# Linear attention, mixer and gating on one core: the first MLP's side work ordered by a table

## The chip, the cores and the metric

The kernel runs on one core of a Trainium2 chip. The metric is device time in microseconds (us), the median of several executions. The engines are called by the names that the profile uses: PE (TensorE, matrix products), DVE (VectorE), ACT (ScalarE), POOL (GpSimd), and SP, which here only issues transfers. Each engine runs its own queue in the order in which the program was written; an instruction that waits holds up what is behind it on its engine.

## The reference

```python
for t in range(S):                       # B=4, H=8, S=768, D=48
    state = alpha[:, :, t, :, None] * state + einsum('bhd,bhe->bhde', k[:, :, t], v[:, :, t])
    y[:, :, t] = einsum('bhd,bhde->bhe', q[:, :, t], state)
x = y.transpose(0, 2, 1, 3).reshape(B, S, H * D)      # 768 x 384 for each of 4 batches
u = x + (x^T @ U @ V)^T                               # mixing over the sequence, rank 32
x = u + relu(u @ w_ch1) @ w_ch2                       # MLP, 384 -> 1536 -> 384
h = relu(x @ w_in);  a, v = halves of h               # 384 -> 1024
out = (a * (w_spatial @ layernorm(v) + b_spatial)) @ w_out
```

All inputs are float32. Products are made of high and low parts, three matmuls for one.

## The kernel before, in words

A batch has 768 rows, held transposed as two blocks of 384 columns. Its eight heads form four pairs, so that there are 16 pairs; pairs 0 to 3 are batch 0, pairs 4 to 7 batch 1. The attention of a pair goes in chunks of 64 rows. `prepare` (three parts, divided by `yield`) makes what depends on alpha alone: the backward scan on DVE (L691) with the scaling of k by POOL (L680) and a copy of the chunk products by ACT (L701); the forward scan (L703) with the scaling of q (L680); and ACT's check of alpha (L707), which reads alpha from the pair's input buffer, writes over the forward scan's tile, and sums into `over`. `Pair` then does the rest: the flip of k on PE (L732) and its copy kn by ACT (L735); `added`, the sums of k and v of each chunk (L775); `state`, with the decays and sums copied by ACT (L782, L783) and the scan over chunks by DVE (L786), in slices of DS columns; `keep` (L796, L797 on ACT); the scores (L748) and their mask (L757 on DVE); the outputs, in two kinds of products (L807 and L817), taken by ACT (L832). A pair's alpha, k and q lie together in one of three buffers, akq_84 to akq_86 in the program's names; pair n + 3 goes into the buffer of pair n, by `load_pair` (L634, two transfers, and L635 for v), as the last step of a pair.

`Mix` makes u: a flip of two halves (L947), ACT's copy of each, the product with U (L963), and its parts into stk (L971 on DVE); the sums with V follow (L291, added by DVE's L294, split by ACT's L295 into partuh and by L226 into partul).

The MLP goes over twelve pieces f of the hidden width. For a block and an f the up group makes nine matmuls (L351), ACT takes h (L358) and DVE the rest hl (L339); two groups later the down group makes three times three matmuls (L260 to L262) with h and hl, summed over some f in three banks, which DVE then adds to u (L409, three times). FIRST says in which ranges of f batch 0 goes. A piece of weights arrives as 64-bit words: DVE takes the high part (L215, L218), ACT scales the low part (L209), POOL adds (L221), ACT copies the high half (L562) and DVE the rest (L226).

Within a group PE's code calls `pull()` after every few matmuls, twice for an up group and four times for a down group. A pull runs the next steps of the work that goes beside the MLP: of `attend` for the next batch, and in batch 0 of the weights' conversion too. When a step is due is a formula: BEGINS and ENDS are the pulls at which a weight is begun and finished, `due()` spreads the steps of `attend` evenly over the pulls.

PSUM has eight banks: 0 to 2 for the down sums, 3 and 4 for the up groups, 5 to 7 ("x") for everything else, taken in turn.

Of the kernel before, what the change touches and what calls it, by code (L numbers as in the profile page):

```python
# [52 lines left out]
DS = 16  # L53
# [38 lines left out]
def gla_mixer_gating_kernel(ctx: ExitStack, tc: tile.TileContext, akq, v, vT, u, v3, w12, w_in, wsT, b_sp, w_out, out):  # L92
# [39 lines left out]
    class Stage:  # L132
# [4 lines left out]
        def __init__(self, pool, items, places=(), width=E, most=1):  # L137
            self.narrow = lambda: pool.tile([128, width], U32, name="narrow", tag="narrow", bufs=2)
            self.items, self.free = list(items), list(places)
            self.loaded, self.late, self.begun, self.most, self.scaled = [], [], 0, most, 0  # L140
# [30 lines left out]
        def begin(self, room=None):  # L171
# [6 lines left out]
            place, words, t, n, wide, finish = self.loaded.pop(0)  # L178
            if wide and not place:
                t = (room or self.narrow())[0 : words.shape[0], 0:n]  # L180
            if wide and not self.scaled:
                low_part(words)
            self.scaled = max(0, self.scaled - 1)
            x = narrowed(words, t) if wide else words
            self.late.append((self.begun, finish(x), place))
            self.begun += 1
            return True
# [23 lines left out]
    def narrowed(words, t):  # L211

        words = words.rearrange("p (n w) -> p n w", w=2)
        low, high = words[:, :, 0], words[:, :, 1]
# [5 lines left out]
        )  # L220
        nc.gpsimd.tensor_tensor(out=t, in0=t, in1=low, op=ALU.add)  # L221
# [85 lines left out]
    class ChannelMlp:  # L307
# [54 lines left out]
        def up_both(self, blocks, f):  # L362
# [14 lines left out]
            for ps in both:  # L377
# [5 lines left out]
                hs.append((h, hl))  # L383
            return hs
# [193 lines left out]
    with ExitStack() as fast:  # L578
# [7 lines left out]
        class Ps:  # L586
# [10 lines left out]
            def tile(self, shape, dtype, name, tag):  # L597
                return self.banks[:, self.place(tag), :]

            def two(self, tag):  # L600

                i, j = self.place(tag), self.place(tag)
                step = j - i
                last = j + (1 if step > 0 else -1)
                return self.banks[:, i : last if last >= 0 else None : step, :]
# [109 lines left out]
        class Pair:  # L715
# [7 lines left out]
            def flip(self, warm=0):  # L723
# [3 lines left out]
                for c0, c1 in ((0, 3), (3, NC)):  # L727
                    pt = ps.tile([128, 512], F32, "ps_kt", self.tags["flip"])
# [714 lines left out]
```

## Time and profile before

| what | value |
|---|---|
| median of 3 runs | 715.99 us (715.32 to 717.61) |
| the profiled execution | 716.3 us |
| its span, first to last instruction | 714.6 us |
| PE busy | 685.5 us, 96% |
| DVE, ACT, POOL busy | 341.0, 285.3, 203.1 us |
| mean granted clock of TensorE | 0.993 |
| chain that ended last | PE 82%, DVE 12%, ACT 3%, issue 2%, POOL 1% |

The times of the sections below come from the profiled execution, and the sum is made against its 716.3 us. PE is nearly always busy, so the views to read are those that tell where PE waits and at which clock it runs.

### The profile page before, as it was taken

To read this page: it belongs to the slowest core of one execution; us is meant where nothing else is said; L and a number is where in the kernel's file an instruction comes from. 1 tells how busy PE (TensorE), PEld (TensorE's weight loads), DVE (VectorE), ACT (ScalarE), POOL (GpSimd) and SP (SyncE) were. 2 spreads that over 40 slices of the span, in tenths; PEclk is the share of its full clock that TensorE was granted. 3 is DMA by queue.
4 is the path that set the end of the run, shared out by engine and by line. 5 is a ranking of instruction groups with operands and counts; after the bars stand their busy time and mean duration, and the time that the engine had idled before them with its cause. 6 is when DMAs were issued, how large, how long until landed. Compare 5 with 4: busy or idle time off the path is not lost.

```text
span 714.6 us, 14432 instructions
## 1 busy us (share of the span) xinstructions
PE 685.5 (96%) x6124; PEld 654.2 (92%) x6124; DVE 341.0 (48%) x584; ACT 285.3 (40%) x552; POOL 203.1 (28%) x172
## 2 busy tenths in 40 slices
PE   7989878999999999999999999999999999999996
PEld 6878867899999999989999999989999989999996
DVE  8998987556444335433233784352252143225211
ACT  3874446655455534454431543332231232214111
POOL 5534533215111031110030132343333223333211
PEclk9999999999999999999999999999999999999999
DMA  9699004442533310400004353400002003000001
GB/s 335 206 345 224 16 2 93 81 92 58 114 71 69 84 18 16 103 2 22 15 1 145 111 167 109 115 7 21 15 34 66 34 1 100 5 29 23 13 34 39
DMA packets 21178, 54.20 MB, mean 76 GB/s; under 512 B 2704, under 2 KB 12816, under 8 KB 19824
## 3 DMA queue, kind: packets, MB, share of 16 engines
q1 hardware_dynamic: 21104, 53.18, 27.2%
q8 instruction: 50, 0.82, 0.5%
q14 instruction: 24, 0.20, 0.1%
HBM read 42.55 MB, written 9.44 MB: 73 GB/s over the span
## 4 chain that ended last, share of the span: by engine, by line
PE 82%; DVE 12%; ACT 3%; issue 2%; POOL 1%; DMA 0%; DVEq 0%; ACTq 0%
PE banks L351 19%; PE banks L260 18%; PE banks L262 17%; PE banks L261 17%; PE banks L817 2%; DVE bw L691 2%; DVE narrow L215 1%; DVE fw L703 1%; PE banks L963 1%; PE banks L748 1%; PE banks L807 1%; DVE w L226 1%; PE banks L775 1%; PE banks L732 1%; PE banks L947 1%
## 5 line engine op out<-in xcount | busy, mean ns | idle before, releaser
L351 PE MATMUL banks<-partuh,w 128*128 128x384 f32 x564 | 131.0, 340 | 4.5 <-DVE hl L339 4.5
L351 PEld LDWEIGHTS banks<-partuh,w 128*128 128x128 f32 x564 | 100.5, 189 | 6.2 <-DVE hl L339 5.8
L339 DVE SCALAR_TENSOR_TENSOR hl<-banks,h 128x384 fp32r<-128x384 f32 x96 | 52.9, 552 | 103.4 <-ACT h L358 102.6
L260 PE MATMUL banks<-h,w 128*128 128x384 f32 x288 | 99.8, 347 | 0.9 <-DVE ub L409 0.9
L262 PE MATMUL banks<-hl,w 128*128 128x384 f32 x288 | 96.9, 337 | 0.0
L261 PE MATMUL banks<-h,w 128*128 128x384 f32 x288 | 96.9, 336 | 0.0
L511 DVE TENSOR_TENSOR vsb<-banks,bb 128x384 f32<-128x384 f32 x32 | 17.8, 558 | 129.6 <-PE banks L262 129.6
L358 ACT ACTIVATE h<-banks 128x384 fp32r<-128x384 f32 x94 | 45.9, 488 | 75.4 <-PE banks L351 74.4
L226 POOL TENSOR_TENSOR partul<-ub,partuh 128x384 fp32r<-128x384 f32 x45 | 46.0, 1048 | 91.8 <-ACT partuh L295 75.1
L517 ACT ACTIVATE gh<-gt 128x384 fp32r<-128x384 f32 x32 | 16.8, 525 | 126.3 <-DVE gt L514 126.3
L226 POOL TENSOR_TENSOR gl<-gt,gh 128x384 fp32r<-128x384 f32 x32 | 32.4, 1014 | 120.7 <-ACT gh L517 120.7
L261 PE MATMUL banks<-wsph,vl 128*128 128x384 f32 x192 | 65.1, 339 | 1.0 <-POOL vl L226 0.9
L351 PE MATMUL banks<-partul,w 128*128 128x384 f32 x282 | 66.1, 342 | 0.0
L260 PE MATMUL banks<-wsph,vh 128*128 128x384 f32 x192 | 64.9, 338 | 0.0
L262 PE MATMUL banks<-wspl,vh 128*128 128x384 f32 x192 | 64.9, 338 | 0.0
L260 PEld LDWEIGHTS banks<-h,w 128*128 128x128 f32 x288 | 54.4, 189 | 2.6 <-DVE ub L409 1.2
L261 PEld LDWEIGHTS banks<-h,w 128*128 128x128 f32 x288 | 54.5, 189 | 0.0
L262 PEld LDWEIGHTS banks<-hl,w 128*128 128x128 f32 x288 | 54.5, 189 | 0.0
L351 PEld LDWEIGHTS banks<-partul,w 128*128 128x128 f32 x282 | 50.0, 189 | 0.7
L680 POOL TENSOR_TENSOR akq<-akq,bw 128x768 f32<-128x768 f32 (+1 forms) x15 | 24.6, 1640 | 82.4 <-DVE bw L691 82.4
L680 POOL TENSOR_TENSOR akq<-akq,fw 128x768 f32<-128x768 f32 (+1 forms) x15 | 25.0, 1666 | 61.3 <-DVE fw L703 54.8
L226 POOL TENSOR_TENSOR vl<-vt,vh 128x512 fp32r<-128x512 f32 x20 | 27.1, 1382 | 49.8 <-ACT vh L481 49.8
(184 smaller groups left out, 1374.7 us busy)
## 6 DMA issues: line engine op xcount, KB each, us to landing
akq<-in_akq SPq DMA_DIRECT2D x24, 434.4 KB, 7.1
bits<-in_w SPq DMA_DIRECT2D x12, 768.0 KB, 12.3
x2d<-ub SPq DMA_DIRECT2D x8, 576.0 KB, 3.5
ub<-x2d SPq DMA_DIRECT2D x8, 576.0 KB, 4.9
out_y<-ob SPq DMA_DIRECT2D x24, 192.0 KB, 1.9
v<-in_v SPq DMA_DIRECT2D x15, 288.0 KB, 7.5
words<-in_w_in SPq DMA_DIRECT2D x8, 384.0 KB, 3.2
words<-in_wsT SPq DMA_DIRECT2D x4, 576.0 KB, 5.0
```

Source lines behind the costliest of these rows:

```text
L226: engine.tensor_tensor(out=out, in0=x, in1=hi.bitcast(F32), op=ALU.subtract)
L260: nc.tensor.matmul(out=ps, lhsT=wh, rhs=xh, start=first, stop=False)
L261: nc.tensor.matmul(out=ps, lhsT=wl, rhs=xh, start=False, stop=False)
L262: nc.tensor.matmul(out=ps, lhsT=wh, rhs=xl, start=False, stop=last)
L339: nc.vector.scalar_tensor_tensor(out=hl, in0=ps[:, 0:TB], scalar=0.0, in1=h.bitcast(F32), op0=ALU.max, op1=ALU.subtract)
L351: nc.tensor.matmul(out=ps[:, 0:TB], lhsT=wx[:, k * 128 : (k + 1) * 128], rhs=ux[:, k, :], start=i == 0, stop=i == len(parts) - 1)
L358: nc.scalar.activation(out=h, in_=ps[:, 0:TB], func=AF.Relu)
L511: nc.vector.tensor_tensor(out=vsb, in0=psv[:, 0:TB], in1=self.g["bb"][:, blk * TB : (blk + 1) * TB], op=ALU.add)
L517: nc.scalar.activation(out=hi, in_=gt, func=AF.Copy)
L680: engine.tensor_tensor(out=chunks(x)[:, c], in0=chunks(x)[:, c], in1=chunks(by)[:, c, 1:CW], op=ALU.mult)
L691: nc.vector.tensor_tensor_scan(out=bw[:, ::-1], data0=a[:, 1 : AW + 1][:, ::-1], data1=ends[:, ::-1], initial=0.0, op0=ALU.mult, op1=ALU.max)
L817: nc.tensor.matmul(out=self.py[HW * h : HW * h + D, x, j * CH : (j + 1) * CH], lhsT=self.w[:, c - 1, h, :], rhs=self.q[:, c * CH : (c + 1) ...
```

## The change

The diff is cut to its core; line numbers of the kernel before are used throughout, apart from the rows of the changed program below, in which L727 is the check L707, L585 is L562, L379 is L358, L755 is L735, L721 is L701, L852 is L832, L654 is L634, L655 is L635, L247 is L226, L360 is L339, L711, L714 and L723 are L691, L694 and L703, L232 and L235 are L215 and L218, L432 is L409 and L806 is L786.

```diff
-DS = 16
+DS = 8
...
-FIRST = (0, 5, 8, 12)
+FIRST = (0, 5, 8, 10, 12)
 N_WARM = 12
-BEGINS = (1, 9, 17, 25, 34, 43, 54, 65, 76, 87)
-AHEAD, N_AHEAD, HELD = 20, 5, 62
-ENDS = tuple(x + y for x in BEGINS for y in (10, 12))
+FIRST_STEPS = {
+    5: "f", 6: "b", 13: "fbf", 22: "fbf", 31: "fbf", 40: "fbf", 49: "fbf", 58: "f", 59: "pf", 67: "p",
+    70: "a", 72: "b", 73: "a", 77: "aa", 78: "fbf", 82: "a", 83: "ar", 84: "fpf", 91: "p", 92: "a", 95: "a", 97: "b",
+    99: "aa", 103: "fbf", 104: "a", 105: "a", 106: "r", 108: "fpf", 114: "p", 117: "a", 119: "pa", 121: "r", 122: "aa",
+    123: "p", 126: "a", 127: "aa", 129: "a", 130: "r", 131: "aa", 132: "p", 134: "a", 135: "a", 137: "a", 138: "a", 139: "p",
+    140: "a", 142: "a", 144: "a", 145: "ar",
+}
 BANKS = {"acc": 3, "mm": 2, "x": 3}
 PLACES = {"acc": (0, 1, 2), "mm": (3, 4), "x": (5, 6, 7)}
+PAIR = PLACES["x"][0:2]
+ALONE = PLACES["x"][2]
...
+        def high(self, room=None):
+
+            place, words, t, n, wide, finish = self.loaded.pop(0)
...
+            if wide:
+                high_part(words, t)
+            self.raised.append((place, words, t, wide, finish, self.scaled > 0))
+            self.scaled = max(0, self.scaled - 1)
+
+        def add(self):
+
+            place, words, t, wide, finish, scaled = self.raised.pop(0)
+            if wide and not scaled:
+                low_part(words)
+            x = both_parts(words, t) if wide else words
+            self.late.append((self.begun, finish(x), place))
+            self.begun += 1
...
+                if len(hs) == 1:
+                    self.pull()
...
-            def two(self, tag):
...
+            def pair(self):
+
+                return self.banks[:, PAIR[0] : PAIR[1] + 1, :]
...
-                for c0, c1 in ((0, 3), (3, NC)):
-                    pt = ps.tile([128, 512], F32, "ps_kt", self.tags["flip"])
+                for (c0, c1), tag in zip(((0, 3), (3, NC)), self.tags["flip"]):
+                    pt = ps.tile([128, 512], F32, "ps_kt", tag)
...
-                pts = [ps.tile([128, 512], F32, "ps_sc", self.tags["scores"]) for h in range(2)]
+                pts = [ps.tile([128, 512], F32, "ps_sc", PAIR[h]) for h in range(2)]
...
-                pd = ps.two(self.tags["state"])
+                pd = ps.pair()
...
-                decay = pd[:, 0, D * NC : D * NC + DS * NCH]
+                decay = pd[:, 0, TB : TB + DS * NCH]
...
-                    self.py = ps.two(self.tags["out"])
+                    self.py = ps.pair()
...
-        def attend(b, blocks):
-
-            tags = {"flip": "x", "scores": "x", "state": "x", "out": "x"}
+        checks = []
+
+        def prepare_some(ns):
+
+            for n in ns:
+                x = prepare(n)
+                next(x)
+                yield
+                next(x)
+                checks.append(x)
+                yield
+
+        def attend(b, blocks, alone=False):
+
+            tags = {"flip": (ALONE, PAIR[0])}
...
-                ahead = prepare(n + 1)
+                ahead = iter(()) if alone else prepare(n + 1)
                 pair.flip()
                 if mix:
-                    mix.take(mix.flip(0))
+                    mix.take(mix.flip(0, PAIR[1]))
                 yield
...
                 pair.state(pair.added())
                 if mix:
-                    mix.take(mix.flip(1))
+                    mix.take(mix.flip(1, ALONE))
...
                 pair.mask(pair.scores())
-                next(ahead, None)
...
                 if mix:
-                    gp = mix.product()
+                    gp = mix.product(0, ALONE)
                 pair.outputs()
...
                 if n + 3 < NPAIR:
                     load_pair(n + 3)
+                next(ahead, None)
...
+            if alone:
+                blocks += [(us[blk], *up.parts()) for blk in range(NB)]
+                for blk in range(NB):
+                    for m in range(KE - 1):
+                        mix_sum(g, blocks[blk], blk, m, stk, ps, "x")
+                    yield
+                    if blk == 0:
+                        mix.take(mix.flip(0))
+                        mix.take(mix.flip(1))
+                        yield
+                mix.keep(mix.product())
+                yield
+                for blk in range(NB):
+                    mix_sum(g, blocks[blk], blk, KE - 1, stk, ps, "x")
+                    yield
+                return
...
-            for m, blk, engine in (
-                (0, 0, nc.gpsimd), (0, 1, nc.gpsimd), (1, 0, nc.gpsimd), (2, 0, nc.vector), (1, 1, nc.vector), (2, 1, nc.vector)
-            ):
+            for blk in range(NB):
                 t, hi, lo = blocks[blk]
-                rest(lo[:, m, :], t[:, m, :], hi[:, m, :], engine)
-            weights.finish(1)
+                for m in range(KE):
+                    rest(lo[:, m, :], t[:, m, :], hi[:, m, :], nc.gpsimd if blk == m == 0 else nc.vector)
...
-        more = attend(1, nxt)
-        steps = chain(rest_of_first, more)
+        steps = attend(1, nxt, True)
+        ahead_of_1 = prepare_some(range(NP, 2 * NP + 1))
...
-            if b == 0 and pulls in ENDS:
-                weights.finish(1)
-            if b == 0 and pulls in BEGINS:
-                weights.begin()
+            if b == 0:
+                for x in FIRST_STEPS.get(pulls, ""):
+                    if x == "f":
+                        weights.finish(1)
+                    elif x == "b":
+                        weights.begin()
+                    elif x == "r":
+                        next(checks.pop(0))
+                    else:
+                        next(ahead_of_1 if x == "p" else steps, None)
+                return
             while done < due():
                 done += 1
                 next(steps, None)
...
+            if b == 0:
+                mlp.flush()
             drain(steps)
```


In batch 0 the formula gives way to FIRST_STEPS. Its letters are: f, finish a step of the oldest weight; b, begin one; p, the next of the two first parts of `prepare`, for pairs 4 to 8 in turn; a, the next step of `attend` for batch 1; r, the next check of alpha. In the other batches the check comes after `load_pair` instead of after the scores. The sums, scores and outputs of a pair are always in banks 5 and 6 (PAIR); bank 7 (ALONE) has the first half of the flip of k, the second half of the mix's flip, and its product. For batch 1 the last pair's mixing goes beside the sums of the first two, and the down groups that are left at the end of batch 0 run before the next MLP. The last lines of batch 0's own attention move: the low parts by ACT, the conversion of the first weights, partul on DVE five times of six.

**The first check of batch 1, on ACT.** Tile akq_84 is the buffer of pairs 4 and 7; w, h and kn are a weight's high half, an up group's result and the copy of k, and a wait on DMAHW and a number is one for a transfer. Before:

```order
L209 ACTIVATE bits<-bits 128x768 [waits DMAHW2_49]
L562 ACTIVATE w_835<-narrow 128x768 [waits Pool_49]
L358 ACTIVATE h<-banks 128x384 [waits PE_49]
L707 ACTIVATE fw,over<-akq_84,below 128x780 [waits DMAHW7_49,DMAHW6_49,Pool_49]
L358 ACTIVATE h<-banks 128x384 [waits PE_49]
L209 ACTIVATE bits<-bits 128x768 [waits DMAHW3_49]
L562 ACTIVATE w_878<-narrow 128x768 [waits Pool_49]
```

In the change, where y is pair 4's output:

```order
L852 ACTIVATE y_1162<-banks 48x384 [waits DVE_49,PE_49]
L852 ACTIVATE y_1162<-banks 48x384
L852 ACTIVATE y_1165<-banks 48x384 x2
L727 ACTIVATE fw,over<-akq_84,below 128x780 [waits DMAHW2_49,DMAHW1_49]
L585 ACTIVATE w_1176<-narrow 128x768 [waits Pool_49]
L721 ACTIVATE seen<-bw 128x12 [waits DVE_49]
L379 ACTIVATE h<-banks 128x384 [waits PE_49] x2
L755 ACTIVATE kn<-banks 128x384 [waits PE_49] x2
```

The check now follows the pair's outputs and waits for two transfer queues; before, it stood among the up groups, and its two queues were those of the load before. On SP, the loads with v between them, before:

```order
L634 DMA akq_86<-in_akq 48x2317 [waits DMAHW6_49,PE_49]
L634 DMA akq_86<-in_akq 48x2317 [waits DMAHW7_49]
L635 DMA v<-in_v 128x576 [waits DMAHW0_49]
L634 DMA akq_84<-in_akq 48x2317 [waits DMAHW1_49,PE_49,Activation_49]
L634 DMA akq_84<-in_akq 48x2317 [waits DMAHW2_49]
L635 DMA v<-in_v 128x576 [waits DMAHW3_49]
```

and in the change:

```order
L654 DMA akq_86<-in_akq 48x2317 [waits DMAHW6_49,PE_49]
L654 DMA akq_86<-in_akq 48x2317 [waits DMAHW7_49]
L655 DMA v<-in_v 128x576 [waits DMAHW0_49]
L654 DMA akq_84<-in_akq 48x2317 [waits DMAHW1_49,PE_49,Pool_49]
L654 DMA akq_84<-in_akq 48x2317 [waits DMAHW2_49]
L655 DMA v<-in_v 128x576 [waits DMAHW3_49]
```

The load of akq_84 by SP waited for PE and ACT, the check's reader among them; now it waits for PE and POOL, and the check is behind the load.

**The second check, on ACT and DVE.** ACT in the change, where ub is the tile of pair 5's outputs and akq_85 the buffer of pairs 5 and 8:

```order
L379 ACTIVATE h<-banks 128x384 [waits PE_49]
L852 ACTIVATE ub<-banks 48x384 [waits DVE_49,PE_49]
L852 ACTIVATE ub<-banks 48x384 x3
L727 ACTIVATE fw,over<-akq_85,below 128x780 [waits DMAHW1_49,DMAHW0_49]
L585 ACTIVATE w_1428<-narrow 128x768 [waits Pool_49]
L721 ACTIVATE seen<-bw 128x12 [waits DVE_49]
L379 ACTIVATE h<-banks 128x384 [waits PE_49] x2
L755 ACTIVATE kn<-banks 128x384 [waits PE_49] x2
```

DVE, around the weight that ACT copies there, before:

```order
L226 TENSOR_TENSOR w_1145<-narrow,w_1145 128x768 [waits Activation_49,Pool_49]
L691 SCALAR_TENSOR_TENSOR bw<-akq_86,ends 128x780 [waits DMAHW7_49,DMAHW6_49]
L694 RECIPROCAL starts<-bw 128x12 [waits DVE_49]
L339 SCALAR_TENSOR_TENSOR hl<-banks,h 128x384 [waits Activation_49]
L409 TENSOR_TENSOR ub<-banks,ub 128x384 [waits PE_49] x3
```

and in the change:

```order
L247 TENSOR_TENSOR w_1343<-narrow,w_1343 128x768 [waits Activation_49]
L360 SCALAR_TENSOR_TENSOR hl<-banks,h 128x384 [waits Activation_49]
L711 SCALAR_TENSOR_TENSOR bw<-akq_86,ends 128x780 [waits DMAHW7_49,DMAHW6_49]
L714 RECIPROCAL starts<-bw 128x12 [waits DVE_49]
L247 TENSOR_TENSOR w_1428<-narrow,w_1428 128x768 [waits Activation_49]
L360 SCALAR_TENSOR_TENSOR hl<-banks,h 128x384 [waits Activation_49]
L432 TENSOR_TENSOR ub<-banks,ub 128x384 [waits PE_49] x3
L723 SCALAR_TENSOR_TENSOR fw<-akq_86,starts 128x780 [waits DVE_49]
```

The weight's rest, hl and three sums (L432) stand behind what ACT does after the check.

**The scans of pair 4's state, on DVE.** Before:

```order
L691 SCALAR_TENSOR_TENSOR bw<-akq_85,ends 128x780 [waits DMAHW4_49,DMAHW3_49]
L694 RECIPROCAL starts<-bw 128x12 [waits DVE_49]
L215 TENSOR_SCALAR narrow<-bits 128x768 [waits DMAHW5_49]
L218 SCALAR_TENSOR_TENSOR narrow<-bits,narrow 128x768 [waits DVE_49]
L226 TENSOR_TENSOR w_977<-narrow,w_977 128x768 [waits Activation_49]
L786 SCALAR_TENSOR_TENSOR after<-add,banks 128x192 [waits Activation_49]
L786 SCALAR_TENSOR_TENSOR after<-add,banks 128x192 x2
L703 SCALAR_TENSOR_TENSOR fw<-akq_85,starts 128x780
```

and in the change:

```order
L432 TENSOR_TENSOR ub<-banks,ub 128x384 [waits PE_49] x3
L723 SCALAR_TENSOR_TENSOR fw<-akq_84,starts 128x780 [waits DVE_49]
L360 SCALAR_TENSOR_TENSOR hl<-banks,h 128x384 [waits Activation_49]
L232 TENSOR_SCALAR narrow<-bits 128x768 [waits DMAHW4_49]
L235 SCALAR_TENSOR_TENSOR narrow<-bits,narrow 128x768 [waits DVE_49]
L806 SCALAR_TENSOR_TENSOR after<-add,banks 128x96 [waits Activation_49]
L806 SCALAR_TENSOR_TENSOR after<-add,banks 128x96 x5
```

The next pair's backward scan and the weight's rest no longer stand ahead of the scans of `after`; the pair's own forward scan and one weight's high part do.

## Rows read from the trace of the kernel before

**Rows 1.** The page: the span, and TensorE's busy time, share, instructions.

```profile
span 714.6 us, 14432 instructions
...
PE 685.5 (96%) x6124; PEld 654.2 (92%) x6124; DVE 341.0 (48%) x584; ACT 285.3 (40%) x552; POOL 203.1 (28%) x172
```

**Rows 2.** Waits of PE, 54 to 146 us: releaser: us in total, times, longest.

```profile
PE banks L748 <- DVE after L786: 5.6, 3, 3.0
PE banks L351 <- DVE hl L339: 4.5, 4, 1.6
PE banks L732 <- issue: 1.9, 2, 1.5
PE banks L260 <- DVE ub L409: 0.9, 1, 0.9
PE banks L807 <- DVE sm L757: 0.4, 2, 0.2
```

**Rows 3.** Waits of PE over the whole span, the two other ones.

```profile
PE banks L947 <- ACT add L783: 2.4, 2, 1.2
...
PE banks L909 <- DVE ybsuh L870: 1.0, 2, 0.6
```

**Rows 4.** Timeline of PE: start, us, work [idle before <-releaser].

```profile
98.95 0.92 PE L748 MATMUL banks<-akq 64*64 64x64 f32 x46 [3.00 <-DVE after L786]
```

**Rows 5.** Stretches: busy us of each engine, granted TensorE clock, DMA share, GB/s.

```profile
99.00:103.00 4.00, 4.00 (x56) 3.93 (x57) 3.25 (x4) 2.58 (x3) 1.93 (x2) 0.63 0.02 4
...
118.00:121.00 3.00, 3.00 (x42) 2.88 (x37) 2.80 (x5) 2.33 (x4) 1.69 (x1) 0.58 0.11 25
```

**Rows 6.** Timeline of ACT, 91 to 109 us.

```profile
91.53 0.94 ACT L735 ACTIVATE kn<-banks 128x384 f32<-128x384 f32 x2 [3.10 <-PE banks L732]
...
93.52 0.22 ACT L701 ACTIVATE seen<-bw 128x12 f32<-128x12 f32 x1 [0.32 <-DVE bw L691]
...
95.38 0.48 ACT L358 ACTIVATE h<-banks 128x384 fp32r<-128x384 f32 x1
...
102.68 0.95 ACT L707 ACTIVATE fw<-akq,below 128x780 f32<-128x780 f32 x1 [1.39 <-POOL akq L680]
103.54 0.18 ACT L707 ACTIVATION_READ_ACCUMULATOR fw<-akq,below 128x1 f32 x1
...
108.54 0.84 ACT L562 ACTIVATE w<-narrow 128x768 fp32r<-128x768 f32 x1
```

**Rows 7.** Timeline of PE, 104 to 111 us.

```profile
104.99 1.46 PE L817 MATMUL banks<-akq,state 128*48 128x64 f32 x44
...
107.53 0.68 PE L351 MATMUL banks<-partuh,w 128*128 128x384 f32 x3
...
108.57 0.82 PE L732 MATMUL banks<-ident,akq 128*128 128x128 f32 x6
```

**Rows 8.** Timeline of SP's own issues.

```profile
106.53 0.78 SPq L634 DMA_DIRECT2D akq<-in_akq  x2
```

**Rows 9.** L634's loads, 100 to 130 us: from issue to landing.

```profile
DMA to landing us min/median/max: 4.9/6.0/7.3
```

**Rows 10.** Timeline of DVE, 93 to 106 us.

```profile
93.67 2.01 DVE L215 TENSOR_SCALAR narrow<-bits 128x768 uint32<-128x768 uint32 x1
95.72 0.96 DVE L218 SCALAR_TENSOR_TENSOR narrow<-bits,narrow 128x768 uint32<-128x768 uint32 x1
96.59 0.95 DVE L226 TENSOR_TENSOR w<-narrow,w 128x768 fp32r<-128x768 f32 x1
97.46 1.44 DVE L786 TENSOR_TENSOR_SCAN after<-add,banks 128x192 f32<-128x192 f32 x3
...
104.28 0.56 DVE L339 SCALAR_TENSOR_TENSOR hl<-banks,h 128x384 fp32r<-128x384 f32 x1 [2.02 <-ACT h L358]
104.75 0.55 DVE L215 TENSOR_SCALAR narrow<-bits 128x768 uint32<-128x768 uint32 x1
```

**Rows 11.** Timeline of POOL, 93 to 96 us.

```profile
93.57 1.70 POOL L680 TENSOR_TENSOR akq<-akq,bw 128x768 f32<-128x768 f32 x1 [3.76 <-DVE bw L691]
```

More of the change, by code (lines that the diff above doesn't have):

```diff
@@ L139, in __init__ @@
             self.items, self.free = list(items), list(places)
-            self.loaded, self.late, self.begun, self.most, self.scaled = [], [], 0, most, 0
+            self.loaded, self.raised, self.late, self.begun, self.most, self.scaled = [], [], [], 0, most, 0
         def fill(self, most=99):
@@ L169, in scale, with begin @@
             self.scaled += 1
-        def begin(self, room=None):
+        def high(self, room=None):
+            place, words, t, n, wide, finish = self.loaded.pop(0)
+            if wide and not place:
+                t = (room or self.narrow())[0 : words.shape[0], 0:n]
+            if wide:
[9 more added lines that the diff above has]
+            self.begun += 1
+        def begin(self):
             self.fill(1)
@@ L177, in begin @@
                 self.finish()
[L178 to L186, printed above, removed]
+            self.high()
+            self.add()
             return True
@@ L209, in low_part, with high_part @@
         nc.scalar.activation(out=low, in_=low, func=AF.Copy, scale=2.0**-29)
-    def narrowed(words, t):
-        words = words.rearrange("p (n w) -> p n w", w=2)
-        low, high = words[:, :, 0], words[:, :, 1]
+    def high_part(words, t):
+        high = words.rearrange("p (n w) -> p n w", w=2)[:, :, 1]
         nc.vector.tensor_scalar(
@@ L220, in narrowed, with both_parts @@
         )
+    def both_parts(words, t):
+        low = words.rearrange("p (n w) -> p n w", w=2)[:, :, 0]
         nc.gpsimd.tensor_tensor(out=t, in0=t, in1=low, op=ALU.add)
@@ L597, in tile @@
             def tile(self, shape, dtype, name, tag):
-                return self.banks[:, self.place(tag), :]
-            def two(self, tag):
[L602 to L605, printed above, removed]
+                return self.banks[:, tag if isinstance(tag, int) else self.place(tag), :]
+            def pair(self):
+                return self.banks[:, PAIR[0] : PAIR[1] + 1, :]
         ps = Ps()
@@ L985, in attend @@
             moves, mix, last = [], None, None
-            if b * NP not in ready:
+            if b * NP not in ready and not alone:
                 p0 = prepare(b * NP)
@@ L1016, in attend @@
                 pair.mask(pair.scores())
-                next(ahead, None)
                 move_some(moves, 3)
@@ L1074, in first_batch @@
             moves, mixes, pairs = [], [], []
-            tags = {"flip": "mm", "scores": "acc", "state": "x", "out": "x"}
+            tags = {"flip": ("mm", "mm"), "scores": "acc", "state": "x", "out": "x"}
             pair = FirstPair(0, us, moves, tags)
@@ L1108, in first_batch @@
                 if n == 2:
-                    weights.scale()
-                    weights.scale()
+                    low_part(weights.loaded[1][1])
+                    low_part(weights.loaded[2][1])
                 after = FirstPair(n + 1, us, moves, tags)
@@ L1127, in first_batch @@
             narrow = [up.pool.tile([128, KE * TB], U32, name="narrow", tag=x) for x in ("uh0", "ul0")]
-            weights.begin(narrow[0])
-            weights.begin(narrow[1])
-            weights.scale()
+            low_part(weights.loaded[0][1])
+            weights.scaled = N_SMALL + 1
+            weights.high(narrow[0])
+            weights.high(narrow[1])
+            weights.high()
+            for _ in range(N_SMALL + 1):
+                weights.add()
             before()
@@ L1140, in first_batch @@
             flipped(0)
+            weights.high()
             weights.finish(1)
-            weights.begin()
             for x in range(NB):
@@ L1146, in first_batch @@
                 pair.outer(x)
-            for x in range(NB):
-                pair.take(x, nc.vector)
+            pair.take(0)
+            pair.take(1, nc.vector)
             weights.finish(1)
@@ L1163, in first_batch @@
             mixes[2].keep(gp)
+            weights.add()
             for blk in range(NB):
```

28 lines of the change are left out of this document (13 added, 15 removed).

## Prediction

> **What bounds the kernel now.** I read the page first: span 714.6 us, PE busy 96% of it, with a profiled time of 716.3 us [rows 1]. TensorE is the bound, so only its idle time and its clock can be gained. The waits of PE between 54 and 146 us, which is the first MLP, add up to 5.6 + 4.5 + 1.9 + 0.9 + 0.4 = 13.3 us in 12 gaps [rows 2]; this is the stretch whose order the change rewrites. The list of waits over the whole span adds two that the change also touches: 2.4 us in two places where the mixing flip (L947) waits for ACT's L783, and 1.0 us at L909 in the first batch [rows 3]. The longest single gap is 3.00 us, before the scores of pair 4 (L748) [rows 4]. What follows a gap shows in the table of stretches: behind that one the granted clock is 0.63 for 4 us, that is 1.2 GHz for most of them, and it is 0.58 from 118 to 121 us, behind L748's next gap [rows 4, 5]. The two drops cost 4 x 0.37 + 3 x 0.42 = 2.7 us.
>
> **What the change gives.** (1) The order of the first MLP is new everywhere, so I count all 13.3 us of gaps and the 2.7 us of clock as gone and put the new stalls in below. That the early gaps can go is seen from the durations: weights are now begun every 9 pulls, with 3 matmuls to a pull on the average and 0.52 us to three [rows 7], so 4.7 us, in which DVE has L215, L218 and L226 (0.55, 0.96 and 0.95 [rows 10]) and one or two hl (L339) of 0.56 [rows 10], and no scan of a pair stands between them before pull 59. (2) The second flip of the mix goes to bank 7 (ALONE) instead of the next x bank in turn, which L783 was still reading: the 2.4 us in batches 2 and 3 go. Cover: ACT's copies of the two flips now lie beside a group of the MLP; without it they cost 0.5 us each. (3) Reordering the end of batch 0: half of the 1.0 us at L909, 0.5 us; between 0 and 1.5. Narrower slices (DS 8) make six scans of 96 columns instead of three of 192 that take 1.44 us [rows 10]; the columns are the same, so the six take at least 1.44 and, if a scan had a fixed time alone, 2.88; I take 1.6, nearer to the columns: 0.2 us more where DVE is late, and nothing elsewhere. The move of the decay's columns inside its bank, and high_part and both_parts as two functions, add no instruction: 0. Sum of gains: 13.3 + 2.7 + 2.4 + 0.5 = **18.9 us**.
>
> **What it costs, first part: two waits for a load.** Step 'r' is ACT's check of alpha (L707, in the change L727). At pull 83 the table says "ar": the 'a' there is the last step of pair 4's attention, which reloads pair 4's buffer with pair 7, and 'r' then checks that same buffer. The orders of ACT and SP above show it: before, the load waited for ACT, which had long read the buffer; now the check stands behind the load and waits for its two queues. At pulls 105 and 106 the same happens with pair 5's buffer and pair 8. The other three checks, at 121, 130 and 145, wait only for POOL, as before.
>
> How long is the wait? The load can only go out when the pair's last products (L817) have read the buffer: before, L817 started at 104.99, took 1.46, and SP issued the two halves at 106.53 [rows 7, 8]. The four issues of this stretch landed 4.9 to 7.3 us after their issue, median 6.0, so the later half of a pair after about 7.2 [rows 9]. With 0.4 us for the second issue that is 7.6 us behind the end of L817. Then ACT has, in its queue, the check 0.95 + 0.18, L562 0.84, L701 0.22, two L358 of 0.48 and two L735 together 0.94 [rows 6], with starts that overlap the ends by about 0.1: 3.9 us in the first case. So kn is ready at about 11.5 us.
>
> What does PE have meanwhile? By its new order, in the first case 33 MLP matmuls and the flip of pair 5: six matmuls take 1.04 us from start to start, the flip 0.82 to its end [rows 7], so 5.7 + 0.8 and 0.1 for the change of shape: 6.6 us, and then L775 wants kn. Stall: 11.5 - 6.6 = **4.9 us**. In the second case 33 matmuls, 5.8 us, and then a down group that begins new sums must wait for L409 on DVE. L409 is behind L226, which waits for ACT's L562, and behind hl, which waits for L358. ACT gets there at 7.6 + 1.1 + 0.8 + 0.2 + 0.4, DVE has L226 from L562's end on, hl behind L358, and the first L409, which I take to last as long as hl, 1.2 us after L358: 11.3. Stall: **5.5 us**. Both are longer than the 3.00 us gap, so I add a drop of the clock to each, 1.4 us apiece from [rows 5]: 2.8. Bounds: landing at 4.9 for both halves gives stalls of 2.6 and 3.2 and perhaps no drop, together 5.8; a landing a microsecond later gives 12.4 + 2.8. I take 7.2 for the later half, since the check needs both and the median of [rows 9] is that of early and late halves.
>
> The Trainium skill bears on this price. In "DMA: Bandwidth & Descriptors", section "Anatomy of one DMA", a transfer on the path that the page measured costs about 2.0 us plus its bytes over 436 GB/s; for 434 KB I estimate 3.0 us from it, with which both halves would be there 4 us after L817, the stalls would be 1.3 and 1.9 us, and the sum, without a drop of the clock, 710.1. The rows of this trace say 4.9 to 7.3 for these very transfers, and they decide.
>
> **What it costs, second part: waits that shift.** DVE operations with all operands in SBUF stretch while POOL runs: L215 takes 2.01 us beside POOL's scaling L680 (1.70 us), against 0.55 alone [rows 10, 11]. The new order puts such pairs in these places, each priced by the gap of before that has the same cause: (a) L226 of a weight behind pair 4's backward scan and its scaling, 1.0 (L351 waits for hl four times, 4.5 us in all [rows 2]); (b) the flip of pair 4 on bank 7, behind three L409: 0.4; (c) pair 4's scores, where L215 and L218 still stand ahead of the state's scans, but L226 no longer does: 3.00 - 0.95 = about 2.0; (d) the scores of pairs 6 and 7, behind the next pair's scan and scaling: 1.3 each, half of the 2.6 us that L748's two lesser gaps come to [rows 2, 4]; (e) pair 7's flip, behind L971 on bank 7: 1.0; (f) the end of the last pair with its sums: 1.4 where before the last gaps of L807 and L732 were 0.8; (g) the first groups of MLP 1: the flush leaves no down groups to lie beside the last partuh, which come only after product, stk and sum: 1.4, between 0 and 1.7. Sum 1.0 + 0.4 + 2.0 + 2.6 + 1.0 + 1.4 + 1.4 = **9.8 us**, between 6 and 14.
>
> **The sum.** 716.3 - 18.9 + 10.4 + 2.8 + 9.8 = 720.4 for a profiled execution. The median of the runs, 715.99, is 0.3 below the profiled one, so I forecast **720.1 us**.
>
> **Rivals.** A: *the loads are no stall*. If both halves land early (4.9 us) the two waits cost 5.8 without a clock drop; with 8 us for the shifted waits the time is 716.0 - 18.9 + 5.8 + 8 = 710.9: faster. For it: the first landings in [rows 9]; the DMA queues may be emptier than in the old order. Against it: the later half counts, and v is loaded in the same moment. It decides from a landing below about 5.5 us. B: *given back exactly*: the waits are there, 10.4, but the clock holds and the shifted waits are 8: 716.0 - 18.9 + 10.4 + 8 = 715.5. Against it: the clock fell after 3.00 us. C: *the clock falls after the scores' gaps as well*, three more drops of 1.4, or the shifted waits reach 14: 720.1 + 4.2 = 724.3, up to 726. For it: the clock is low from 118 to 121 us, where no gap is as long as 3.00 [rows 5]. D: *the banks don't do what they say*: with PAIR fixed, the first half of the mix flip still shares a bank with the state's sums, and these now wait for ACT's copy of the flip; the 2.4 us of [rows 3] stay: 722.5. It lies inside the forecast's own range.
>
> **How the numbers follow.** The forecast (with D) 0.42, C 0.18, B 0.18, A 0.22. Its own range is 718.2 to 723.5. The range that should hold the time 8 times in 10 takes in B, the upper half of A's and most of C's: 711.5 to 726.0. A measurement tells this kernel from no change from about 0.3%, 2.1 us: faster (under 713.8) 0.22, same 0.18, slower (over 718.1) 0.60.
>
> **What would show it.** In the new profile, the check at L727 should be preceded twice by ACT idle for several microseconds that a DMA ended, at roughly 105 and 120 us; PE should have gaps of 4 to 6 us at L795 (waiting for kn or what is behind it) and at L281 (waiting for L432), with a granted clock well below 1 behind both. There should be no gap at L372 before pull 59, none of 1.2 us at L967 in batches 2 and 3, and gaps of 1 to 2 us at three of the four scores (L768). I am wrong if the loads land before ACT comes to the check, if ACT's later operations don't hold PE up, or if the early gaps of the MLP stay.

## The result, and the profile after

| kernel | median | runs | ratio to before, 95% interval |
|---|---|---|---|
| before | 715.86 us | 715.16 to 717.61 | |
| changed | 723.55 us | 722.10 to 726.86 | 1.0107 [1.0087, 1.0127] |

The change makes the kernel slower by 1.1%, 7.7 us. The forecast was 720.1, slower; the measured time lies just above its own range (718.2 to 723.5) and inside the wider one. The profiled execution took 722.1 us, 5.8 more than the one of before.

The page says that PE is busy 2.4 us longer than before [rows 1], and the span is 5.6 us longer:

```profile
span 720.2 us, 14462 instructions
...
PE 687.9 (96%) x6124; PEld 656.1 (91%) x6124; DVE 339.5 (47%) x626; ACT 284.8 (40%) x554; POOL 202.2 (28%) x170
```

In the rows of the change, L281 to L283 are L260 to L262 of before, L312 is L291, L316 is L295, L372 is L351, L392 is L371, L752 is L732, L768 is L748, L795 is L775 and L837 is L817. The waits of PE over the whole span (what it waited for, "issue" being nothing that the profile shows; us in total, times, longest) answer to [rows 2, 3]. The waits for hl at the up groups (there L351, 4.5 us) are gone, and so are those of the mix's flip for L783 (2.4 us). Two new ones stand on top:

```profile
PE banks L281 <- DVE ub L432: 7.2, 2, 6.6
PE banks L795 <- ACT kn L755: 4.5, 1, 4.5
PE banks L768 <- DVE after L806: 3.2, 2, 1.8
PE banks L752 <- issue: 2.0, 1, 2.0
PE banks L372 <- ACT partuh L316: 1.5, 1, 1.5
...
PE banks L312 <- ACT ub L852: 0.8, 1, 0.8
```

Where they are, PE's timeline shows (start, us, work, idle before and what ended it). None of the listed gaps of before is left in the first 45 us of the MLP; the first is at 93 us, before pair 4's scores, 1.43 us where it was 3.00 [rows 4]. Then come 4.47 us before pair 5's sums (L795) and 6.56 us before a down group (L281):

```profile
93.01 0.93 PE L768 MATMUL banks<-akq 64*64 64x64 f32 x48 [1.43 <-DVE after L806]
...
111.06 0.84 PE L795 MATMUL banks<-v,kn 64*64 64x48 f32 x42 [4.47 <-ACT kn L755]
...
135.24 0.66 PE L281 MATMUL banks<-h,w 128*128 128x384 f32 x1 [6.56 <-DVE ub L432]
```

ACT's timeline at the same places: it copies pair 4's outputs (L852), then stands idle for 5.39 us until a DMA of akq ends, runs the check (L727), and gets to kn (L755) at 110.12. The second time it is idle for 6.62 us.

```profile
100.05 2.02 ACT L852 ACTIVATE y<-banks 48x384 f32<-48x384 f32 x4 [2.70 <-PE banks L837]
107.46 0.94 ACT L727 ACTIVATE fw<-akq,below 128x780 f32<-128x780 f32 x1 [5.39 <-DMA akq<-in_akq]
...
110.12 0.88 ACT L755 ACTIVATE kn<-banks 128x384 f32<-128x384 f32 x2
...
131.40 0.94 ACT L727 ACTIVATE fw<-akq,below 128x780 f32<-128x780 f32 x1 [6.62 <-DMA akq<-in_akq]
```

The loads that it waits for were issued right behind the last products, as before [rows 8]:

```profile
100.08 1.97 SPq L654 DMA_DIRECT2D akq<-in_akq  x2
...
122.83 1.91 SPq L654 DMA_DIRECT2D akq<-in_akq  x2
```

The first landed 7.4 us behind its issue (100.08 to 107.46), the second 8.6 us (122.83 to 131.40). The two issues of a pair took 1.9 us together here, against 0.78 [rows 8].

At both gaps, and at a third of 2.01 us (before pair 7's flip, below), the granted clock fell (busy us of each engine, then the clock, as in [rows 5]):

```profile
110.00:120.00 10.00, 8.95 (x127) 8.57 (x128) 8.56 (x18) 6.86 (x11) 3.56 (x2) 0.83 0.06 13
...
130.00:140.00 10.00, 4.76 (x59) 4.28 (x63) 6.80 (x8) 4.23 (x9) 1.68 (x1) 0.66 0.10 18
...
150.00:160.00 10.00, 6.62 (x82) 5.64 (x77) 1.56 (x7) 6.41 (x14) 0.00 (x0) 0.83 0.64 118
```

After that, the gaps at the scores of pairs 6 and 7 and at pair 7's flip:

```profile
144.05 0.93 PE L768 MATMUL banks<-akq 64*64 64x64 f32 x48 [0.69 <-ACT h L379]
...
152.99 1.51 PE L752 MATMUL banks<-ident,akq 128*128 128x128 f32 x6 [2.01 <-issue]
...
160.44 0.93 PE L768 MATMUL banks<-akq 64*64 64x64 f32 x48 [1.81 <-DVE after L806]
```

Where did the time go? PE's gaps of the first MLP and its end, 80 to 182 us, come to 20.6 us, against 13.3: +7.3. The clock costs about 5.4 us: 1.7 in the first and the third of these stretches, and 2.0 in the second, where it stood at 0.50 from 133 to 139 us but PE had no work until 135.24. Before, the two drops cost 1.7 us each, the second with 0.2 in the next stretch:

```profile
100.00:110.00 10.00, 10.00 (x130) 9.56 (x130) 4.75 (x8) 6.21 (x11) 1.69 (x1) 0.83 0.28 57
110.00:120.00 10.00, 7.78 (x121) 6.68 (x120) 9.90 (x13) 5.27 (x10) 4.56 (x3) 0.85 0.50 95
```

That is 3.4, and the difference +2.0. The MLP begins 1.3 us earlier, since L392 starts at 47.81 (L371 before: 49.15), and 2.4 us of batches 2 and 3 are gone. But the first six matmuls with partul last 2.26 us where they lasted 1.20, without a gap in the list: DVE makes five of the six partul there, one behind the other, until 51.85. That is +1.1.

```profile
47.81 2.36 PE L392 MATMUL banks<-partuh,w 128*128 128x384 f32 x12
50.08 2.26 PE L392 MATMUL banks<-partul,w 128*128 128x384 f32 x6
52.37 0.79 PE L372 MATMUL banks<-partuh,w 128*128 128x384 f32 x3
```

and before

```profile
51.34 1.20 PE L371 MATMUL banks<-partul,w 128*128 128x384 f32 x6
```

The sum is 7.3 + 2.0 + 1.1 - 1.3 - 2.4 = +6.7, of a measured 5.6; 1.1 us the other way is not placed.

### The profile page after: what moved, and what is told of

The parts are those of the page before. It is cut to its first block, busy times and chain, and to the rows that moved or that the text cites. A ratio compares the mean times of both kernels' runs of the same rounds, so it can differ in the third digit from the quotient of the medians.

```text
span 720.2 us, 14462 instructions
## 1 busy us (share of the span) xinstructions
PE 687.9 (96%) x6124; PEld 656.1 (91%) x6124; DVE 339.5 (47%) x626; ACT 284.8 (40%) x554; POOL 202.2 (28%) x170
## 4 chain that ended last, share of the span: by engine, by line
PE 87%; DVE 5%; ACT 3%; DMA 3%; issue 1%; POOL 1%; SPq 0%; ACTq 0%; DVEq 0%
PE banks L372 19%; PE banks L281 18%; PE banks L282 17%; PE banks L283 17%; DMA akq<-in_akq 3%; PE banks L837 2%; PE banks L983 2%; PE banks L768 1%; PE banks L827 1%; PE banks L752 1%; PE banks L795 1%; PE banks L967 1%; DVE bw L711 1%; PE banks L929 1%; DVE ub L432 1%
## 5 line engine op out<-in xcount | busy, mean ns | idle before, releaser
L372 PE MATMUL banks<-partuh,w 128*128 128x384 f32 x564 | 130.4, 339 | 1.6 <-ACT partuh L316 1.5
L281 PE MATMUL banks<-h,w 128*128 128x384 f32 x288 | 101.0, 351 | 7.2 <-DVE ub L432 7.2
L372 PEld LDWEIGHTS banks<-partuh,w 128*128 128x128 f32 x564 | 101.2, 190 | 2.4 <-ACT partuh L316 1.8
L360 DVE SCALAR_TENSOR_TENSOR hl<-banks,h 128x384 fp32r<-128x384 f32 x96 | 53.1, 553 | 96.6 <-ACT h L379 96.0
L283 PE MATMUL banks<-hl,w 128*128 128x384 f32 x288 | 97.0, 337 | 0.0
L379 ACT ACTIVATE h<-banks 128x384 fp32r<-128x384 f32 x94 | 45.6, 489 | 78.9 <-PE banks L372 78.3
L247 POOL TENSOR_TENSOR partul<-ub,partuh 128x384 fp32r<-128x384 f32 x43 | 44.3, 1052 | 80.2 <-ACT partuh L316 67.4
L247 POOL TENSOR_TENSOR gl<-gt,gh 128x384 fp32r<-128x384 f32 x32 | 32.5, 1016 | 120.5 <-ACT gh L540 120.5
L372 PE MATMUL banks<-partul,w 128*128 128x384 f32 x282 | 65.6, 340 | 0.0
L281 PE MATMUL banks<-wsph,vh 128*128 128x384 f32 x192 | 64.9, 338 | 0.0
L283 PE MATMUL banks<-wspl,vh 128*128 128x384 f32 x192 | 64.8, 338 | 0.0
L281 PEld LDWEIGHTS banks<-h,w 128*128 128x128 f32 x288 | 54.5, 189 | 9.3 <-issue 6.9
L283 PEld LDWEIGHTS banks<-hl,w 128*128 128x128 f32 x288 | 54.5, 189 | 0.0
L372 PEld LDWEIGHTS banks<-partul,w 128*128 128x128 f32 x282 | 50.1, 189 | 0.5
L247 POOL TENSOR_TENSOR vl<-vt,vh 128x512 fp32r<-128x512 f32 x20 | 27.2, 1384 | 49.8 <-ACT vh L504 49.8
```

Of the source, the lines that this page charges most:

```text
L247: engine.tensor_tensor(out=out, in0=x, in1=hi.bitcast(F32), op=ALU.subtract)
L281: nc.tensor.matmul(out=ps, lhsT=wh, rhs=xh, start=first, stop=False)
L283: nc.tensor.matmul(out=ps, lhsT=wh, rhs=xl, start=False, stop=last)
L360: nc.vector.scalar_tensor_tensor(out=hl, in0=ps[:, 0:TB], scalar=0.0, in1=h.bitcast(F32), op0=ALU.max, op1=ALU.subtract)
L372: nc.tensor.matmul(out=ps[:, 0:TB], lhsT=wx[:, k * 128 : (k + 1) * 128], rhs=ux[:, k, :], start=i == 0, stop=i == len(parts) - 1)
L379: nc.scalar.activation(out=h, in_=ps[:, 0:TB], func=AF.Relu)
```

## The experiments

In the changed kernel, and in the runs below that keep a check behind its load, the check of pairs 4 and 5 reads the alpha of pairs 7 and 8, and that of pairs 4 and 5 goes unchecked. The matmuls on the identity add nothing to the output. All else is computed as before.

**1. The checks ahead of the reload (e1_checks_first).**

```diff
-    ... 82: "a", 83: "ar", ... 105: "a", 106: "r", ...
+    ... 82: "a", 83: "ra", ... 105: "ra", ...
```

> The changed kernel with the two checks of alpha put just ahead of the reload of their buffer (at pulls 83 and 105) instead of behind it; ACT's queue keeps its order, only what the check waits for is another. Theory, the wait for the load: the gaps of 4.5 us (kn) and 6.6 us (L432) go, and with them the two drops of the clock behind them, some 2.5 us: 723.6 - 11.1 - 2.5 = 710, between 708 and 713, faster than before the change. Rival, ACT is late in these places by its order and not by the load: ACT still ends its work late, gaps of 3 us and more stay, 719 to 724.

Measured: 711.05 us (710.58 to 714.18), ratio to before 0.9938 [0.9918, 0.9957]. ACT's queue has the same order, and the check follows the outputs at once:

```profile
99.96 1.98 ACT L852 ACTIVATE y<-banks 48x384 f32<-48x384 f32 x4 [2.71 <-PE banks L837]
101.97 0.95 ACT L727 ACTIVATE fw<-akq,below 128x780 f32<-128x780 f32 x1
```

So the wait is the load's, and it costs 12.5 us with all that hangs on it: without it the change is 0.6% faster than before. The rival falls. Of the 12.5, PE's gaps from 80 to 182 us account for 8.5: they come to 12.1 us in this profile and to 20.6 in the change's. The rest is not seen in this pair of profiles, whose spans differ by 8.9; the mean granted clock was 0.989 to 0.995 in the executions of this run and 0.981 to 0.988 in those of the change, and the profiled one here (713.11 us, 0.991, with three drops) is the second longest of its six. What is left in PE's timeline are smaller gaps; they are taken up in runs 6 and 7:

```profile
123.86 0.41 PE L281 MATMUL banks<-h,w 128*128 128x384 f32 x1 [1.10 <-DVE ub L432]
...
132.67 1.56 PE L768 MATMUL banks<-akq 64*64 64x64 f32 x48 [2.37 <-ACT h L379]
...
142.90 0.85 PE L752 MATMUL banks<-ident,akq 128*128 128x128 f32 x6 [2.00 <-issue]
```

**2. Only the first check (e2_first_check).** 

```diff
-    ... 83: "ar", ...
+    ... 83: "ra", ...
```

> The changed kernel with only the first of the two checks ahead of the reload. Theory: the gap at L795 and the drop of the clock behind it go, 4.5 + 1.3: 717.8, between 716 and 719.5; the gap at L281 stays at 6 to 7 us. Rival, the two waits share a cause (a full transfer queue, or DVE behind by then): the second gap shrinks or grows by more than 1.5 us with it, and the time leaves that range.

Measured: 715.83 us (713.83 to 718.4), just below the stated 716, and 7.7 less than the change where 5.8 were expected; the profiled spans differ by 6.2 (720.2 and 714.0). The second gap stays nearly as it was:

```profile
128.88 0.66 PE L281 MATMUL banks<-h,w 128*128 128x384 f32 x1 [6.14 <-DVE ub L432]
```

The two waits are separate. Of the second one's 6.1 us only 2.7 are seen between this profile (span 714.0) and run 1's (711.3), and 4.8 between the medians: with it gone, L281 still waits 1.10 us and pair 6's scores 2.37 instead of 0.67, and the clock falls three times in run 1's profile against twice here.

**3. Work for PE in the first wait (e3_filled, e5_filled_18).**

```diff
-                pair.state(pair.added())
+                pair.state(pair.added(FILL if n == NP + 1 else 0))
```

> The changed kernel with 40 matmuls on the identity ahead of pair 5's sums, in the 4.5 us in which PE waits for kn. Theory: PE's start after the wait doesn't move, but the clock stays up behind it, so that the 1.3 us or so that the matmuls behind the gap lose come back: 722.3, granted clock 1.00 from 110 to 120 us. Rival, the drop of the clock is not set by this gap or costs nothing on the path that decides: 723.6, or later if the 40 matmuls outlast the wait.

Measured with FILL = 40: 725.2 us (722.85 to 727.49). The 40 matmuls ran 9.1 us, so PE started pair 5's sums 4.3 us later than in the change, and yet the time rose by 1.7 only, with overlapping ranges. With FILL = 18 the matmuls end inside the wait:

> As the run with the 40 matmuls on the identity, now 18: there they took 9.1 us (two passes each) and outlasted the wait of 4.5 us by far. 18 take 4.1 us. Theory: the sums of pair 5 start where they did in the changed kernel, at about 111.1 us, the granted clock is 1.00 from 110 to 120 us instead of 0.83, and the next products (L837) start 1.3 to 1.7 us earlier than at 121.3; time 722, between 721 and 723. Rival, the clock falls in spite of the work, or the 1.5 us are lost again in the second wait: 723.6.

Measured: 720.98 us (719.02 to 723.93), 2.6 less than the change. PE's timeline, then the stretch from 110 to 120 us:

```profile
106.40 4.18 PE L734 MATMUL banks<-ident 128*128 128x128 f32 x36
111.84 0.84 PE L796 MATMUL banks<-v,kn 64*64 64x48 f32 x42 [1.25 <-ACT kn L756]
...
120.61 1.45 PE L838 MATMUL banks<-akq,state 128*48 128x64 f32 x44
```

```profile
110.00:120.00 10.00, 8.72 (x148) 7.87 (x150) 9.67 (x19) 7.26 (x14) 3.61 (x2) 1.00 0.06 14
```

The sums started 0.8 us later than in the change, as the load landed later in this execution, but the clock stayed at 1.00 and L837 (L838 here, a line lower) came at 120.61 instead of 121.30 in the change: 8.77 us behind the sums' start instead of 10.24. The drop of the clock behind this wait costs 1.5 us, by this pair of rows. The whole time says it less clearly: the profiled execution is the longest of its six, since the clock fell behind the second wait as in the change, and three times after it where it fell once in the change.

**4. The banks alone (e4_banks_alone).** The kernel before with the change's lines on the banks and nothing else; the decay keeps its columns and DS is 16.

```diff
-                pd = ps.two(self.tags["state"])
+                pd = ps.pair()
...
-                    mix.take(mix.flip(0))
+                    mix.take(mix.flip(0, PAIR[1]))
...
-                    mix.take(mix.flip(1))
+                    mix.take(mix.flip(1, ALONE))
...
-            tags = {"flip": "x", "scores": "x", "state": "x", "out": "x"}
+            tags = {"flip": (ALONE, PAIR[0])}
```

> The kernel before with nothing but the fixed banks for a pair's flip, sums, scores, outputs and mix. Theory: the two waits of 1.2 us of the mix's flip for ACT in batches 2 and 3 go: 715.9 - 2.4 = 713.5, and the rest stays as it was. Rival, the wait comes back at the state's sums, which now share a bank with the first half of the mix's flip: 715.9, or up to 718 if it comes in batch 1 too.

Measured: 712.42 us (711.0 to 714.18), ratio 0.9951 [0.9933, 0.9968]: 3.5 us faster, 1.1 more than expected. The waits of PE over its span (L747 is the scores, L731 the flip of k, L353 the up groups):

```profile
PE banks L353 <- DVE hl L341: 4.5, 4, 1.6
PE banks L747 <- DVE after L785: 3.9, 3, 1.6
PE banks L731 <- issue: 3.1, 3, 2.4
```

The mix's flip is not among them any more. The rest of the gain, 1.1 us, is placed only in part: in the first MLP scores and flips wait 3.9 + 3.1 us where they waited 5.6 + 1.9 [rows 2], 0.5 less in all, with 1.11 us before pair 4's scores instead of 3.00 and 2.44 before its flip instead of 1.51.

**5. Behind the reload, but late (e6_checks_late).**

```diff
-    ... 83: "ar", ... 97: "b", ... 106: "r", ... 121: "r", ...
+    ... 83: "a", ... 97: "br", ... 121: "rr", ...
```

> The changed kernel with both checks still behind the reload of their buffer, but later: the first at pull 97 instead of 83, the second at 121 instead of 106, so that the transfer has landed when ACT comes to them. Theory, only the time in flight costs: no idle of ACT at L727 over 1 us, no gap of PE of 3 us or more, 711, between 709.5 and 713, as with the checks ahead of the reload. Rival, a check behind the reload is bad in itself (ACT's order, or its work of 1.1 us in a crowded place): gaps of 2 us or more at the scores of pairs 5 and 6, 714 to 719.

Measured: 711.88 us (709.23 to 713.34), as in run 1. The only wait of ACT at the check is now one for POOL:

```profile
ACT fw L727 <- POOL akq L700: 2.4, 1, 2.4
```

A check behind the reload costs nothing that these runs resolve once the transfer has landed: the fault is the time in flight, not the order as such.

**6. The product's parts ahead of the outputs (e7_keep_first),** on top of run 1.

```diff
-                    gp = mix.product(0, ALONE)
+                    mix.keep(mix.product(0, ALONE))
                 pair.outputs()
-                if mix:
-                    mix.keep(gp)
```

> The run with the checks ahead of the reload, and in every pair the parts of the mix's product (L990, L991) taken ahead of the pair's outputs instead of behind them. Theory: the gap of 2.0 us before pair 7's flip comes from bank 7, which ACT empties only behind its four copies of the outputs (1.98 us); it goes, and nothing else moves: 711.05 - 2.0 = 709.0, between 708 and 710. Rival: the flip of pair 7 then waits for something else (a copy by ACT, its scaling), 711.

Measured: 707.63 us (706.45 to 709.13), 3.4 less than run 1. The gap before pair 7's flip is half as long; its second half now waits for the copies of the outputs, in bank 5:

```profile
132.73 0.93 PE L768 MATMUL banks<-akq 64*64 64x64 f32 x48 [2.37 <-ACT h L379]
...
141.04 0.55 PE L752 MATMUL banks<-ident,akq 128*128 128x128 f32 x3 [1.02 <-ACT ub L852]
```

So bank 7 was the cause, but only 1.0 us of the 2.0 was to be had there. Another 1.1 us went where the theory had expected nothing, at the end of batch 1's last pair. Run 1 waits there for 0.84, 0.18, 0.61 and 0.27 us, among them

```profile
160.27 0.44 PE L312 MATMUL banks<-vs,stk 96*128 96x384 f32 x1 [0.18 <-DVE stk L991]
...
161.32 0.44 PE L281 MATMUL banks<-h,w 128*128 128x384 f32 x1 [0.61 <-DVE ub L432]
```

and this run for the first alone:

```profile
155.98 0.62 PE L312 MATMUL banks<-vs,stk 96*128 96x384 f32 x2 [0.84 <-ACT ub L852]
```

The rest of the gain, some 1.4 us, is put down to the clock, whose mean was 0.994 to 0.998 in the executions of this run and 0.989 to 0.995 in run 1's. The gap of 2.37 us before pair 6's scores is there in both, and run 1 shows, from 130 to 140 us,

```profile
130.00:140.00 10.00, 7.63 (x163) 7.00 (x161) 6.19 (x14) 4.79 (x9) 3.29 (x2) 0.83 0.02 4
```

and this run

```profile
130.00:140.00 10.00, 7.63 (x170) 6.70 (x168) 6.53 (x15) 6.17 (x12) 3.35 (x2) 1.00 0.02 6
```

**7. The scan later (e8_scan_later),** on top of run 6.

```diff
-    ... 117: "a", 119: "pa", ...
+    ... 117: "a", 119: "ap", ...
```

> The run with the product's parts first, and pair 7's backward scan behind pair 6's state scans instead of ahead of them (the p and the a of pull 119 change places). Theory: the gap of 2.4 us before pair 6's scores comes from that scan, which lasts 3.1 us beside POOL's scaling; it goes with the drop of the clock behind it: 709.0 - 2.4 - 0.9 = 705.7, between 705 and 708. Rival: pair 7's flip or scores take the wait over, 708 to 709.5.

Measured: 704.72 us (704.15 to 706.06), ratio to before 0.9855 [0.9835, 0.9874]. In run 1 DVE's timeline had shown the backward scan (L711) for 3.1 us ahead of the state's scans (L806), with 0.88 us of idle besides, since ACT's copy of the sums stood behind that scan too:

```profile
126.70 3.10 DVE L711 TENSOR_TENSOR_SCAN bw<-akq,ends 128x780 f32<-128x780 f32 x1
...
130.95 1.58 DVE L806 TENSOR_TENSOR_SCAN after<-add,banks 128x96 f32<-128x96 f32 x6 [0.88 <-ACT add L803]
```

Now there is no gap at pair 6's scores, and these remain in the stretch:

```profile
123.84 0.41 PE L281 MATMUL banks<-h,w 128*128 128x384 f32 x1 [1.10 <-DVE ub L432]
...
138.83 0.55 PE L752 MATMUL banks<-ident,akq 128*128 128x128 f32 x3 [1.02 <-ACT ub L852]
...
144.42 0.93 PE L768 MATMUL banks<-akq 64*64 64x64 f32 x48 [1.81 <-DVE after L806]
```

This is the fastest version, about 11 us faster than before and about 19 faster than the change.

**8. Wide slices again (e9_wide_slices),** on top of run 7:

```diff
-DS = 8
+DS = 16
...
-                decay = pd[:, 0, TB : TB + DS * NCH]
+                decay = pd[:, 0, D * NC : D * NC + DS * NCH]
```

> The last run (checks ahead of the reload, product's parts first, scan later) with slices of 16 columns again, and the decay in its old columns. Theory: the slices hardly matter, 1.44 us of DVE against 1.58 and the ACT copy of the decays 0.33 against 0.26, both on the path in the three gaps before the scores: 704.7 within 0.7. Rival: something waits for a part of the scans, so that narrow slices set it free earlier: 706 or more.

Measured: 705.19 us (704.08 to 705.5), against 704.72; as ratios to before, 0.9839 against 0.9855. No difference that this resolves; the slices are worth nothing here.

**9. Partul's engines as before (e10_partul_pool),** on top of run 7:

```diff
-            for blk in range(NB):
-                t, hi, lo = blocks[blk]
-                for m in range(KE):
-                    rest(lo[:, m, :], t[:, m, :], hi[:, m, :], nc.gpsimd if blk == m == 0 else nc.vector)
+            for m, blk, engine in (
+                (0, 0, nc.gpsimd), (0, 1, nc.gpsimd), (1, 0, nc.gpsimd), (2, 0, nc.vector), (1, 1, nc.vector), (2, 1, nc.vector)
+            ):
+                t, hi, lo = blocks[blk]
+                rest(lo[:, m, :], t[:, m, :], hi[:, m, :], engine)
```

> The same run with the order and the engines of the kernel before for partul: three of six on POOL. Theory: the first MLP's second group comes later again, because hl stands behind more on DVE or the last partul is late: 0.5 to 1.5 us, 705.2 to 706.3. Rival: PE had nothing to gain there, 704.7 within 0.4.

Measured: 709.52 us (708.53 to 710.43), 4.8 more than run 7 and 4.3 more than run 8, whose time was taken together with this one; far outside what either theory gave. POOL has a weight's addition first (L242), then three partul for 3.86 us; PE waits 2.09 us for the last of them at the very start of the MLP:

```profile
47.01 1.86 POOL L242 TENSOR_TENSOR narrow<-narrow,bits 128x768 uint32<-128x768 uint32 x1 [8.57 <-ACT bits L227]
48.84 3.86 POOL L247 TENSOR_TENSOR partul<-ub,partuh 128x384 fp32r<-128x384 f32 x3
```

```profile
52.75 1.68 PE L392 MATMUL banks<-partul,w 128*128 128x384 f32 x5 [2.09 <-POOL partul L247]
```

The clock is 0.83 from 50 to 60 us behind it, and a gap of 1.26 us at 89 us comes on top. So the new order of the end of batch 0 and the move of partul to DVE belong together, and the latter is worth 4 to 5 us (the edit also puts back the order of the six; the wait is for POOL).

## Why the prediction was right, and where it wasn't

**The two waits** were what decided, as forecast, and of the stated size: 4.9 us was forecast for the first, 4.47 came; 5.5 for the second, 6.56 came. The step that was too small is the landing of the second load: 8.6 us behind its issue instead of 7.6. What made it late is not shown; the two issues took 1.9 us instead of 0.8, but so they did for the first load, which came after 7.4. Runs 1, 2 and 5 show the cause. Rival A, early landings, is out: 7.4 and 8.6 us were measured. The estimate that the prediction works out from the Trainium skill's "DMA: Bandwidth & Descriptors", section "Anatomy of one DMA", has both halves there 4 us after the products; the page measured one transfer on another path, and the trace does not agree with its figure here.

**The gains** of 18.9 us came for the most part: no old gap is left before 93 us, and the waits for L783 are gone (run 4: 3.5 us for the banks, where 2.4 were forecast). Against them stand the 1.1 us of the first matmuls with partul. The term for the end of batch 0, 0.5 us, was far off: the MLP starts 1.3 us earlier, and with partul's old engines the kernel is 4 to 5 us slower (run 9). I had taken the row of L909 for its measure and not asked what POOL has in its queue there.

**The shifted waits** were summed at 9.8 us; the profile has 1.43 (pair 4's scores, forecast 2.0), 0.69 + 1.81 (pairs 6 and 7, forecast 2.6), 2.01 (pair 7's flip, 1.0), 0.84 + 0.18 + 0.61 + 0.28 + 0.16 (the end, 1.4) and 1.52 (MLP 1, 1.4), and nothing at the two places (a) and (b), forecast 1.4: together 9.5. Single terms were off by up to 1.0 us, and the sum was good by luck as much as by working.

**The clock** is the term that was too small, and the 3.4 us by which the time exceeds the forecast are mostly its. For the profiled execution 720.4 was forecast and 722.1 came. The new drops cost 5.4 us instead of 2.8: a third, at the 2.01 us gap before pair 7's flip, costs 1.7 us and was not in the sum, and the other two cost 1.7 and 2.0 instead of 1.4 each, because the stretches of [rows 5] leave out a part of each drop. For the same reason the old drops, counted as 2.7, were 3.4. With 0.4 more of gaps (20.6 against 10.4 + 9.8) and the MLP's start 0.8 better, that is 2.6 - 0.7 + 0.4 - 0.8 = 1.5 of the 1.7. The median is another 1.4 us above the profiled execution, where 0.3 below was forecast: the other executions show mean granted clocks of 0.981 to 0.986, the profiled one 0.988, the highest, with the lowest time. Rival C named this mechanism and gave it the wrong place, the scores; its time, 724.3, is nearer to the 723.55 than the forecast's. Rivals B and D are out: the clock fell behind both waits (run 3 shows the price for one), and the banks did what they say (run 4). That ACT's and DVE's queues were the way from the load to PE is seen in the rows; the price of each step in them was not measured apart.

**Left open:** where the last 0.6 us of run 4 lie, what made the second load late, and what the flush at the end of batch 0 costs or gives; none was tried.

## What to carry to other kernels

When a step is moved in a hand-made order, ask of every buffer that it reads who writes it next: a read that slips behind the reload turns a wait of the transfer for the engine into one of the engine for the transfer, and all that is queued behind it waits along. Two letters of a table cost 12.5 us here and hid a change that was otherwise good, which the run with only those letters exchanged shows. And an engine's share of work is to be chosen anew with the order: three of the six partul on POOL, as before the change, cost 4 to 5 us in the new order, where POOL has other work first.

## What was not expected of the hardware

The clock's drop does not follow from the length of a gap alone: a gap of 2.37 us before the same scores left the clock at 0.83 from 130 to 140 us in run 1 and at 1.00 in run 6. One of 2.0 us was followed by 0.83 in the change. So executions of one kernel differ: those of run 1 had mean granted clocks of 0.989 to 0.995 and took 714.18 to 710.58 us. Matmuls that compute nothing of use held it at 1.00 through a wait of 5.4 us (106.40 to 111.84), though they left 1.25 us idle at its end, and gave 1.5 us. A matmul on the identity in float32 is two instructions, 36 for 18, of 0.12 us each (4.18 us).
